# A mixer kernel in one launch: weight pieces in two transfers, a small score chunk on 128 queries, and a new order

## Chip, cores and metric

The kernel runs on one core of one Trainium2 chip. The metric is the device time of one execution in microseconds (us). One core has five engines that run beside each other, each in the order of its own instructions: TensorE (PE, matmuls; its weight loads are listed as PEld), VectorE (DVE), ScalarE (ACT), GpSimd (POOL) and SyncE (SP, which here only issues transfers, "DMAs"). They wait for each other by semaphores. PSUM is the memory that PE writes to; it has 8 banks.

## What is computed

Four batches of 448 tokens of width 768 go through causal attention with 12 heads of 64, then a token and channel mixer, then a gated unit:

```python
scores = where(causal, (q @ k.T) / 8, -1e9)            # 4 x 12 heads, 448 x 448
x = softmax(scores) @ v                                # to (4, 448, 768)
u = x + (relu(x.T @ w_tok1) @ w_tok2).T                # 448 -> 256 -> 448, over tokens
x = u + relu(u @ w_ch1) @ w_ch2                        # 768 -> 1536 -> 768
h = relu(x @ w_in); a, v = halves(h)                   # 768 -> 1024
v = (v - mean(v)) / sqrt(var(v) + 1e-6)
out = (a * (w_spatial @ v + b_spatial)) @ w_out        # 512 -> 768
```

All of the mixer's weights arrive as 64-bit floats and are narrowed to 32 bits on the chip.

## The kernel before

Two heads make a pair; there are 24 pairs, six to a batch. `scores(n)` multiplies the queries and keys of pair n in four chunks of queries, 0 to 64, 64 to 192, 192 to 320 and 320 to 448, each against the keys up to its end; the two heads lie on the two halves of the 128 rows of PE and run side by side. Pairs 0 to 5 (`whole`) multiply in float32 straight from the loaded `stage`; the others split queries and keys into a high and a low part (`qh`, `ql`) and take three products. DVE subtracts the row's maximum and masks, ACT takes the exponential and its sum, DVE the reciprocal, POOL scales; PE transposes the result (`transposed`), ACT or DVE copies it out of PSUM (`PT`), and `weighted(n)` multiplies by the values into `pso`, which ACT or DVE copies into U. After every third pair `token_mix` transposes half of a batch's U (`psm<-ident,U`, steps x0 to x3), splits it (`xs`) and runs the two token products.

The channel weights are 24 pieces of 128 x 768 numbers (`wch`, units of `UNITS`). `convert` loads a piece from DRAM as 64-bit words into one of three buffers (`way`); `narrow` turns it into float32 in three DVE steps for each half of 384 columns, through a PSUM bank; the result goes back to DRAM (`plain`), and `load_unit` fetches it again, when its use comes near, into one of four buffers (`whl`), where ACT and POOL split it into a high and a low part. The first three pieces are split straight from `way`. Batches 0 and 1 use these units one by one (`ch1`, `ch2`); batches 2 and 3 go together, by seven products in place of eight (`channel_pair`, `seven`). The gated unit's last step, `project`, also uses `seven`: for each block of outputs, products o = 0 to 6 that accumulate in three PSUM banks; what stands in a bank after each is copied or added into the `gate` buffers (`gather`), and finished blocks are stored (`out_t<-gate`, L1397).

Nothing of this runs in the order of the source. Each step is a `job` with its engine, a planned duration, what it reads and writes, a priority, and for PE an extra (`lead`); a search, which is not in the file, has used these numbers to order the jobs, and the file holds only its result: `ORDER` has a place for each job, with one bit that moves it to its other engine (ACT or DVE), and `BANKS` the PSUM bank of each product. `Plan.order` replays that table. The planned durations themselves are read by nothing at run time. So an edit of a duration shows only through the table.

The last product of all is cut in two:

```python
if tail and o == 6 and z == len(us) - 1:
    for half, c in enumerate(HALVES):
        job("PE", 0.66, partial(mms, c=c), ...)
        done(z, o, ps, half)
```

and at the start two filler matmuls on the mask (L1427) keep PE at work while the first softmax is under way.

Of the kernel before, what the change touches and what calls it, by code (L numbers as in the profile page):

```python
# [35 lines left out]
for q in range(4):  # L36
# [44 lines left out]
    "UISkPZv(soz5~AlU;||Xf&+sCVFO|VWCMf)$OFp*%maY~ivx@UmjjpsnFE>wn*-tl`2+d`h6A?)xC6NZodcc&p99SU<^%l${sWu?)C1K6)&s!<!UN6&*8>3r1q22J#RJ&`+5_7I+ymVM=>zHm4FoU*"
    "F$CBHJ_J7mKm_mu^#k?;K?FhsUIbqR3IGfM4FD4W6aWwa5daqe82}sr9sm{q7yuFg6#yCl9RMHzBLE)&CjcS<DgY$_CIB@6L;yDcKL8E@o&aM2WB^3~Mu0#7L4ZO4Ljausp@16zApj%*DF844I{+>K"
    "EC4tFG5{z5F#t9IJOD2MEdV(HGXO^bN&ra!OaM&)P5?*%SO7}^D*)91v;eh$ZUAq9f&ha6gaCzr#sJ3v1^`b0SpZT1Rsd80Pyk#2U;tkLS^!f3R{&K2Q2<^5VE|$PTL5qXaR7DzcK~t#bpUe!cmQ+&"
    "T>$$4u>iAxp8%kMuK=)sq5z`+`2hL=0RaL50|74qFaa?E{s8{~00A5U9RW)LL;+3#Q2}ZJG675hO#xy7i~)@SlmV3im;spq2moaOc>rnvXaHsaYyf=#dH{O>e*kL$X#i&cZ2*A)d;o?3fB=;MnE;yr"
    "oB)^rmjIRkngGxMegGB$(*V=}$N<Rz(E!o_$^gp%6af_hhXAAihyaWLi2#lOrvRn^ssN<`iU5rOivW)RtpKb5s{p6~)&SQ4+W^@B-T>SH-2mDE*Z`>jb^!zd1p)j3{QxZiE&)#gPyuuSbpf^jya2iY"
    "!vMJew*bNby#T-fzW}=c%m6b1xBxT(#Q?+r!2mS@IsrHVHvv2WHUT{WIRQHXz5uTQcL8|;cmbRNodKQ!t^u=wv;nmN-2t`%w*k!oxB<BV&;iZ?&jH^7-T~kN^8xe$^#S$)_W}3;5CRbb2?7cN6ap0j"
    "t^mydvH%MK&j1er4FL=R4gvT87Xb+Y9sxxG69GX1Mgc+r7y$|a9|3Cta{+7tash7vaRF`tZ2@or&H&i~qXDG>q=B#jvH`IH*a7kZ1_1{F-vBBBAOS}KD*;IXECC|{UI9`8ApuAMLjg(wQ~_WCUjb7A"
    "A_2Vt!~w$r!U4Yl!2!hqz5&1i2mu@d`2qR?`vLp`{sH{~8Uh;v5CIVZV*!N$XaQ#dW&vaYrUAwQh5?8H+5yr5X#r&crvb?UhXK(6=>h5i>jCcp>;dfo@B!`t@c|M6R{|sgCITe_O9D&+Py$f`RRV+p"
    "g#v~GfdYa8g92{?Z~}1xegc02fC9q;!~(?v$pXIuzyiSn!UD?z=>p6G`U1)V^#VQtKLMWs#{mukp#h))CjvbJ9Re!?DFP1yq5-@CC;~nL9s(=^Dgr+OMFK+tLIOboMgm6yL;^qpKmo@BYyxe9ZUUnM"
    "r2?b^#sbI!i2;fMVFFD8W&&gaX98jZhXPXqP6AH?XaZ#d-vVO-hyqpuR02{0-~!_U<pSga<^tgY=K|;g;sT2S90T_P_yYL?5d#tf69XCp8w1Dz$^oVVuL7z9tpcb5rvkGAvI4gPumY?Ct^%n7s{*zH"  # L90
    "wF1!sv;yt|@d85w^a33N@&fPz^8)Vz4FWv`9s?kQ9|J@KM*~I!N&`#-O#@B?PXkZ`Q3F&1QUg;1RRdN7R|8lBYXfWpZ3Auta077zbpv(-dIP5ecmt9HcLR9?ngW{w6ax_i7y~2&76TOn7X%sv6a*6l"
    "83QE)7Xy|9A_N-*6$BOpBLpV|Bm^l0B?K!3CIl)3C<L4We*{+qS%g>wWdvu0XoP+QfP}FExB^83G6YKlNCQa&lLI&eHUu*SIRqR8zynAGlmj~iHv~KcIs{1sPXtQ@O$1B?N(4~^P6SW{xdN{Qmjsvu"
    "ngoFaf&_zvtpu)w5(F3oW(02pZ3JrscLZq!cm#0-as+b(ZUk%ujRa~0c?5O@djxa@js%tjl?0Fkk_40lkpzzflLQ$A^#sBM!vw?x%LL2>&V=0r<pkyg=LF~k=>+No>jVx34+Rhf5d{(j69qK|HU&2Y"
    "I0aM%RRvZBR|Sd%iv{)t_XW@e(FHUFH3XRip#+`;pah!)oCK%@rv#$}r39Y@tOU6Podl``sRX11rUbeKzXZDkzy!Pm!36dMy#&4ldITT^2n7rU3x)Rt`2_d`9t9r-a0GP()&$K2*97bY*aX@H)CAK6"
    "(FD%~+yw0e*#z4J)dc$l(ge^1`~?0400jgE0tEpD0|oyC{RD{w#|0t<BLyS{SOr-HS_N+fbA_S=s{{!J76lvyJOwNT3I!Pj7X>B-8U-B%Jq0ZVE(IY47zHN<8wEZELIp+zL<K(uLj^?zKm|bs`UK<!"
    "a0PM&bp>|?fCY91bOm??aRq?|f(3*Hg9W7p;{^Z)G6qZrO$G%91_lQP0R{pF0|o>J2nHqwP6kf~VFqFbPzHtuhX#lSG6ypUzXret)&|!GIR!ceTLobST?J|dUIknQZ3ScnWd&jdU<GRhYz1EhZUtur"
    "W(8vfrUkJDs0FJ9uLY+Cv<0dKtOYv-I0mx?sRgnHum!gTwgt5Xtp%<HxCP|}=LO~k=mj(eQHC!CFa?qYn+1~vmj##wl?9yzp9P!+paql#ngy8!mIa;#qXnS_qy^~(?*;P(@dfw=>jmls76$GGF$J3j"
    "@CEe+^ac3^@&)V#?FASH7X}*!HU>8aH3m`!mIj;#Xa#8n(goTD)dklD(*@K8+XdeR;04_U)&<xFIR^g)+y&wV;RW6WItDxjKL$MpLIyhqMg~3xL<YtM(gs5YK?XnuU<OGBNCrm+Y6e9HYX+AFnFg2!"
    "ng-7X(1rsC1P28N-3HzU-v-(S+XmbQ4+jtj5eGO2IR`oiI|nugHwQciJqJz)PX|>8RtH1}MF*k<2?h`b3kDMgS_TmY6$T6j4h9+q83q&vTLuyabOsFu4+b*^Wd?Nyeg=64cLsq5cm{d~d<J#~3I+=Y"
    "od$gde+GgEfCh~Qdj^9Btp=_J)CSWA)dtZ91_um>Fa|LO#s*3T$Og;?$_B><Xa-{jYzA!x$p*~^&IZc{X$E8l<OXgA<p$~o@CNP%><04&=LYBo<_7Bq@&@q+?*{b-^acS3=?3iv0tW~O2L}oV2?s|9"  # L100
    "RELBHg$AAmrv{(~p$4A@q6Vl2s|K$Iu?D6FqXwl0qz0)5tOl?K6bBUt7zZ8)B?lJ=76%#!AO|7`83!K+AqOT090wZ*9S0)^BnKx4Ne4;?O$SH^X$NWtaR+q=b_Z++Z3k`#cL#U}c?W9;ZwGJ(iwBGc"
    "jR%eghX;rUi3f@Ypa-D`m<O2$)d$)KjscGWmI0Rm+X37G5&{zf3jz!R76LK?HUc*SNCHU$N&<2Ma{_b%bpmz*d;)y}i~@}U%>pd~E&?+GGy*jOodTW$p8}u)p#tgx>jLZo?E(Y?CIcq}F9R?G&I0xV"
    "1p@~IEdwqCJOe!gJ_A1kX9H*hX#<S|jsuSakpry*p#!1=qXVP^rUSAAvjcPkl>@p1-UGV>y#vMr#{<Iy!~@9#$^+j6-~-_U;{)Ua<pbvf=mYTs@&o?^00aUA_XGF?3<M4Y4+IbdECekCLj*(wE(9+G"
    "U<6?VMg&I$V+3RbiUf=V#{|d(w*<HZ$^?7_eFXah`~&j?^aBF~1O!|JT?ASLTLeV}umrIL;{@ac1qB8L2L)mT#RSF#^91w+G6gdQGzE(UM+Ha)j0KGajs=eekp;;F6a^IpP6bZ|Pz6#2Qw0qLdj)(2"
# [136 lines left out]
def mixer_kernel(ctx: ExitStack, tc: tile.TileContext, qkv, wtok, wch, wgv, wsp, bsp, out):  # L241
# [145 lines left out]
    def nominal(n):  # L387
        return 0.0 if n < EAGER else START + (n - EAGER) * STEP
# [1141 lines left out]
```

## Time and profile before

| what | us |
|---|---|
| median of 3 runs (lowest, highest) | 756.04 (755.39, 758.48) |
| the profiled execution | 756.18 |
| its span, first to last instruction | 754.4 |
| PE busy | 741.0 (98%) |
| DVE busy | 635.8 (84%) |
| ACT busy | 419.4 (56%) |
| POOL busy | 293.0 (39%) |
| transfers: 122.06 MB, mean 162 GB/s | |

Busy time is the time in which at least one instruction of an engine runs. Matmuls overlap, so what one costs on PE is the distance from its start to the next one's start, not its duration. Idle time is listed beside the instruction that ended it, with what it had waited for ("<-").

### The profile page before, as it was taken

Reading aid. Unit: us, or ns where it says so; the run is one execution under the profiler, and the core shown is the slowest. Engines: PE = TensorE matmul, PEld = TensorE weight load, DVE = VectorE, ACT = ScalarE, POOL = GpSimd, SP = SyncE. Lnnn points to the kernel's source line nnn. Section 1 sums busy time; section 2 is a strip of 40 time slices with the busy share of each in tenths; the row PEclk is TensorE's granted clock in tenths of the full one; section 3 lists DMA queues with packets and bytes.
Section 4 is the critical chain, followed back from the end, with each engine's and each line's share of the span. In section 5 each row is a group of like instructions: output and inputs, shape, how many; then the busy total and the mean of one; then the engine's idle time right before and its main releaser. Section 6 shows DMA issues by size and latency. Waiting matters only on the chain. (4 is left out here: it accounts for less than half of the span.)

```text
span 754.4 us, 12904 instructions
## 1 busy us (share of the span) xinstructions
PE 741.0 (98%) x4450; PEld 635.6 (84%) x4450; DVE 635.8 (84%) x1529; ACT 419.4 (56%) x1025; POOL 293.0 (39%) x361
## 2 busy tenths in 40 slices
PE   9999999999899999999999999999999999999998
PEld 4667888789778888888799999999888988889997
DVE  6999999988797787776599889999999998789773
ACT  6998665243577865553246567545465655554441
POOL 5789647234695767736120000000430112542600
PEclk9999999999999999999999999999999999999999
DMA  6458879879677879797624402223201011200123
GB/s 246 144 197 283 264 250 325 294 249 330 230 248 242 258 257 341 216 274 221 208 91 141 144 2 84 84 103 129 76 23 43 0 43 50 85 0 13 49 98 135
DMA packets 48754, 122.06 MB, mean 162 GB/s; under 512 B 4912, under 2 KB 20400, under 8 KB 48176
## 3 DMA queue, kind: packets, MB, share of 16 engines
q1 hardware_dynamic: 48688, 121.23, 48.7%
q8 instruction: 35, 0.57, 0.3%
q14 instruction: 31, 0.25, 0.1%
HBM read 91.46 MB, written 29.75 MB: 161 GB/s over the span
## 5 line engine op out<-in xcount | busy, mean ns | idle before, releaser
L298 PE MATMUL psf<-fb,fa 128*128 128x448 f32 (+1 forms) x422 | 154.6, 366 | 1.1 <-DVE U L1091 0.6
L300 PE MATMUL psf<-fb,fa 128*128 128x448 f32 (+1 forms) x422 | 154.4, 366 | 0.1
L299 PE MATMUL psf<-fb,fa 128*128 128x448 f32 (+1 forms) x422 | 154.4, 366 | 0.0
L289 POOL TENSOR_TENSOR whl<-whl 128x768 fp32r<-128x768 f32 x45 | 82.9, 1852 | 102.3 <-ACT whl L818 82.0
L488 ACT ACTIVATE P<-P,stats 128x320 f32<-128x320 f32 (+3 forms) x192 | 96.0, 503 | 31.4 <-DVE stats L471 30.5
L509 POOL TENSOR_SCALAR P<-P,stats 128x320 f32<-128x320 f32 (+3 forms) x192 | 87.4, 473 | 29.9 <-DVE stats L500 26.2
L298 PEld LDWEIGHTS psf<-fb,fa 128*128 128x128 f32 x422 | 79.2, 188 | 9.2 <-issue 1.0
L937 ACT CAST fa<-raw 128x384 fp32r<-128x384 f32 (+1 forms) x112 | 55.9, 531 | 54.0 <-DVE raw L951 23.6
L300 PEld LDWEIGHTS psf<-fb,fa 128*128 128x128 f32 x422 | 79.3, 188 | 7.4 <-DVE fa L289 0.4
L299 PEld LDWEIGHTS psf<-fb,fa 128*128 128x128 f32 x422 | 79.3, 188 | 7.3
L471 DVE CUSTOM_DVE_ANT_0 P<-pss,mask 64x64 f32<-64x64 f32 (+3 forms) x192 | 70.2, 413 | 9.6 <-PE pss L462 8.8
L289 POOL TENSOR_TENSOR wv<-wf,wv 128x512 fp32r<-128x512 f32 x6 | 8.5, 1425 | 154.0 <-ACT wv L1167 154.0
L289 DVE TENSOR_TENSOR fa<-raw,fa 128x384 fp32r<-128x384 f32 (+1 forms) x109 | 59.7, 572 | 5.2 <-ACT fa L937 4.6
L298 PE MATMUL ps<-hid,whl 128*128 128x448 f32 x144 | 54.2, 376 | 0.0
L818 ACT CAST whl<-whl 128x768 fp32r<-128x768 f32 x45 | 37.0, 832 | 30.4 <-DMA whl<-plain 28.8
L300 PE MATMUL ps<-hid,whl 128*128 128x448 f32 x144 | 52.8, 367 | 1.0 <-POOL whl L289 1.0
L298 PE MATMUL ps<-uhl,whl 128*128 128x448 f32 x144 | 53.6, 372 | 0.0
L300 PE MATMUL ps<-uhl,whl 128*128 128x448 f32 x144 | 52.7, 366 | 0.0
L299 PE MATMUL ps<-uhl,whl 128*128 128x448 f32 x144 | 52.7, 366 | 0.0
L299 PE MATMUL ps<-hid,whl 128*128 128x448 f32 x144 | 52.7, 366 | 0.0
L901 ACT CAST fb<-U 128x448 fp32r<-128x448 f32 x57 | 31.5, 565 | 27.6 <-DVE U L906 16.6
L289 POOL TENSOR_TENSOR ql<-stage,qh 128x896 fp32r<-128x896 f32 x18 | 38.1, 2120 | 7.6 <-ACT qh L396 7.2
(182 smaller groups left out, 1786.7 us busy)
## 6 DMA issues: line engine op xcount, KB each, us to landing
way<-in_wch SPq DMA_DIRECT2D x24, 768.0 KB, 6.3
whl<-plain SPq DMA_DIRECT2D x45, 384.0 KB, 5.2
stage<-in_qkv SPq DMA_DIRECT2D x23, 448.0 KB, 4.2
plain<-way SPq DMA_DIRECT2D x24, 384.0 KB, 5.0
raw<-plain SPq DMA_DIRECT2D x24, 384.0 KB, 3.6
round<-PB SPq DMA_DIRECT2D x7, 1024.0 KB, 6.1
PT<-round SPq DMA_DIRECT2D x28, 256.0 KB, 5.2
v<-in_qkv SPq DMA_DIRECT2D x24, 256.0 KB, 4.6
```

Of the source, the lines that this page charges most:

```text
L289: e.tensor_tensor(lo, x, hi.bitcast(F32), op=ALU.subtract)
L298: nc.tensor.matmul(ps, ah, bh, start=(first and i == 0), stop=False, **kw)
L299: nc.tensor.matmul(ps, ah, bl, start=False, stop=False, **kw)
L300: nc.tensor.matmul(ps, al, bh, start=False, stop=(last and i == n - 1), **kw)
L471: nc.vector.tensor_tensor_reduce(out=P(i)[:M, j, :], in0=ps(i, j), in1=mask[:M, S - 128 : S - 128 + W] if j == 0 and n < BLOCKS or M == 64 ...
L488: nc.scalar.activation(P(i)[:M, j, :], P(i)[:M, j, :], AF.Exp, bias=s.t[:M, 0, c : c + 1], scale=-1.0, accum_out=sums(s)[:M, c, 0:1])
L509: nc.gpsimd.tensor_scalar(P(i)[:M, j, :], P(i)[:M, j, :], s.t[:M, 1, c : c + 1], 1.0, op0=ALU.mult, op1=ALU.mult)
L818: job("ACT", act(DM, False), lambda: nc.scalar.copy(w.t[:, 0, :], w.t[:, 1, :].bitcast(F32)), r=ks, w=ks, prio=p)
L901: job("ACT", act(S, False), lambda: nc.scalar.copy(f(0), x_()), r=wk, w=[(h, k, 0)], prio=p)
L937: job("ACT", act(n, False), lambda: nc.scalar.copy(part(o, 0), at(d)), r=[key(d)], w=[wk], prio=p + 0.1 * o)
```

## The change

1. `wch` is laid out as two contiguous halves of 384 columns per piece, and `convert` loads a piece of channel weights in two transfers, one for each half (768 KB becomes 2 x 384 KB). The narrowing of a half now depends on its own transfer alone. Both transfers wait until both halves of the buffer's last contents have been narrowed (`ends`). The token weights' pieces stay whole.
2. In the pairs with float32 scores the chunk of 64 queries is multiplied with 128 queries (`wide`): 64 rows of the result are not read by anything.
3. The last product is whole again, and only ACT's copy of it and its store are cut in halves.
4. Planned durations and leads of the score jobs and of some transposes are lowered, and the search was run again: `ORDER` and `BANKS` are new throughout. 32 jobs take their other engine in place of 38; six copies go from DVE to ACT. The transfers rise from 307 to 331.

```diff
 ORDER = (
-    "4*&oF0RRF31ONj71po&C@Br}u^Z*(G8v*M8>;UZm?f~xq2>>(zIslLWkpPqc;sE0S<pAaY83B?2lK|iV;Q-_S3jpT;=m6;e>HzWp^#Jw&BmpJ?Cjs{WC;=$}RRMzmgaK9oR{>Z7Spi)ETmka{TLEDK"
+    "4*&oF0RRF31ONj71po&C?f~xq^Z*wD83E}4>HzBi>;UZm2>>(zegLTessOD3-~izO;{fCUG6AaqtN`8s-vHtO3jpN+<^bma=m78l^#Jw&9|0l(BLVjS4FMzpB>`3eR{>Z7SpixBTLD}FVF6$P@c<41"
...
 BANKS = (
-    "777777777777777777777773333333333333333333333333333333345021354654021354655021346654544546564021364566021366655021364566645464654021354545021375645021"
+    "777777777777777777777773333333333333333333333333333333345021356555021366455021346454464556645021354646021356454021365466654464546021354545021364574021"
...
-    def narrow(d, dk, w, wk, n, prio, banks=(3,)):
+    def narrow(d, dk, w, wk, n, prio, banks=(3,), ends=()):
...
-            job("DVE", (n * 1.04 + 70) / 1e3, lambda k=k: step(k), r=[dk, (ps, 0)] if k else [dk], w=[wk] if k == 2 else [(ps, 0)], touch=[wk[0]], prio=prio)
+            job("DVE", (n * 1.04 + 70) / 1e3, lambda k=k: step(k), r=[dk, (ps, 0)] if k else [dk], w=[wk, *ends] if k == 2 else [(ps, 0)], touch=[wk[0]], prio=prio)
...
-        n = src.shape[-1]
-        dk = (b, "d")
-        job("SP", 0.385, lambda: nc.sync.dma_start(b.t[:, : 2 * n], src.bitcast(U32)), w=[dk], prio=prio, size=n * 1024, lead=0.29 if n == DM else 0.415)
+        if isinstance(src, tuple):
+            for k, x in enumerate(src):
+                job("SP", 0.385, lambda k=k, x=x: nc.sync.dma_start(b.t[:, 2 * HALF * k : 2 * HALF * k + 2 * HALF], x.bitcast(U32)), r=[(b, "ends", x) for x in (False, True)], w=[(b, "d", k)], prio=prio + 0.1 * k, size=HALF * 1024, lead=0.34)
+        else:
+            n = src.shape[-1]
+            job("SP", 0.385, lambda: nc.sync.dma_start(b.t[:, : 2 * n], src.bitcast(U32)), w=[(b, "d", 0), (b, "d", 1)], prio=prio, size=n * 1024, lead=0.29 if n == DM else 0.415)
...
-        def ps(i, j):
+        def ps(i, j, wide=False):
             k, o_ = PLACE[i]
-            M, W = CHUNKS[i][1] - CHUNKS[i][0], CHUNKS[i][1]
+            M, W = 128 if wide else CHUNKS[i][1] - CHUNKS[i][0], CHUNKS[i][1]
...
+                wide = whole and i == 0
+                if wide:
+                    q1 = 128
...
-        for some, us in (((3, 0), 1.214 if whole else 0.86), ((2, 1), 1.065 if whole else 0.86)) if n else (((0, 1), 1.1), ((3,), 0.85), ((2,), 0.85)):
+        for some, us, lead in (((3, 0), 1.075 if whole else 0.776, 0.0 if whole else 0.08), ((2, 1), 0.97 if whole else 0.838, 0.0 if whole else 0.02)) if n else (((0, 1), 1.0, 0.0), ((3,), 0.85, 0.0), ((2,), 0.85, 0.0)):
...
-        convert(i % 3 if i < 6 else 1 + i % 2, wch[i], parts, LOW + i, (7,) if i < 8 else (3,), keep=i)
+        convert(i % 3 if i < 6 else 1 + i % 2, (wch[i, 0], wch[i, 1]), parts, LOW + i, (7,) if i < 8 else (3,), keep=i)
...
                 if tail and o == 6 and z == len(us) - 1:
-                    for half, c in enumerate(HALVES):
-                        job("PE", 0.66, partial(mms, c=c), r=[us[z][1](o), *((*place[o][i][:2], x) for i in range(n) for x in range(2)), *([("tail", 0)] if half else ())], w=[(ps, half), ("tail", half)], prio=base + 0.01 * o)
+                    for half in range(2):
                         done(z, o, ps, half)
...
+    wch = wch.reshape(24, 128, 2, HALF).transpose(0, 2, 1, 3)
```

How the table moves PE's instructions is shown at three places (a row is a line, an operation, output<-inputs by their names, and the output's size; x2 is two alike in a row). First PE at the scores of pairs 2 and 3 (`stage_145` and `stage_149` are their operands, `pst` a bank of transposes). Before:

```order
L462 MATMUL pss<-stage_145 128x448 x2
L462 MATMUL pss<-stage_145 64x64 x2
L462 MATMUL pss<-stage_145 128x320 x2
L462 MATMUL pss<-stage_145 128x192 x2
L547 MATMUL pst<-ident,P_69 128x128 x2
L547 MATMUL pst<-ident,P_187 128x128 x2
L462 MATMUL pss<-stage_149 128x448 x2
L462 MATMUL pss<-stage_149 64x64 x2
L547 MATMUL pst<-ident,P_70 128x128
L547 MATMUL pst<-ident,P_212 128x128 x3
```

The same place on PE now:

```order
L468 MATMUL pss<-stage_145 128x448 x2
L468 MATMUL pss<-stage_145 128x64 x2
L468 MATMUL pss<-stage_145 128x320 x2
L468 MATMUL pss<-stage_145 128x192 x2
L468 MATMUL pss<-stage_149 128x448 x2
L468 MATMUL pss<-stage_149 128x64 x2
L553 MATMUL pst<-ident,P_187 128x128 x4
L468 MATMUL pss<-stage_149 128x320 x2
L468 MATMUL pss<-stage_149 128x192 x2
```

The small chunk's output grew from 64 x 64 to 128 x 64, and pair 3's first scores now follow pair 2's without transposes between them.

Second, PE at the last token mix of the second batch (`pso` is the weighted product of the batch's last pair, `U_1178` and `U_1184` the batch's U, `ps_2056`, `ps_2108` and `ps_2152` banks of channel products). Before:

```order
L679 MATMUL pso<-PT,v 64x384 x2
L679 MATMUL pso<-PT,v 64x64 x2
L684 MATMUL pso<-PT,v 64x384 x2
L684 MATMUL pso<-PT,v 64x256 x2
L684 MATMUL pso<-PT,v 64x128 x2
L740 MATMUL psm<-ident,U_1178 64x128 x3
L740 MATMUL psm<-ident,U_1178 128x128 x9
L298 MATMUL ps_2056<-uhl,whl 128x448
```

The same place on PE now:

```order
L690 MATMUL pso<-PT,v 64x384 x2
L690 MATMUL pso<-PT,v 64x256 x2
L690 MATMUL pso<-PT,v 64x128 x2
L298 MATMUL ps_2108<-hid,whl 128x448
L299 MATMUL ps_2108<-hid,whl 128x448
L300 MATMUL ps_2108<-hid,whl 128x448
...
L746 MATMUL psm<-ident,U_1184 128x128 x9
L746 MATMUL psm<-ident,U_1184 64x128 x3
L298 MATMUL ps_2152<-uhl,whl 128x448
```

A channel product of nine matmuls now stands between the weighted product and the transposes of what it makes.

Third, the end of PE's order, with buffer numbers (`psf_7971` is, before and after, the bank whose product o = 6 is the one with two copies). Before:

```order
L300 MATMUL psf_8082<-fb_7799,fa_7459 128x448
L298 MATMUL psf_7971<-fb_7980,fa_7449 128x224
L299 MATMUL psf_7971<-fb_7980,fa_7449 128x224
L300 MATMUL psf_7971<-fb_7980,fa_7449 128x224
L298 MATMUL psf_7971<-fb_7999,fa_7449 128x224
L299 MATMUL psf_7971<-fb_7999,fa_7449 128x224
L300 MATMUL psf_7971<-fb_7999,fa_7449 128x224
...
L1526 UNCONDITIONAL_BRANCH
```

The end of PE's order now:

```order
L300 MATMUL psf_7971<-fb_8018,fa_7469 128x448
L298 MATMUL psf_8074<-fb_7843,fa_7479 128x448
...
L300 MATMUL psf_8074<-fb_7830,fa_7479 128x448
L298 MATMUL psf_8021<-fb_7843,fa_7479 128x448
...
L300 MATMUL psf_8021<-fb_7830,fa_7479 128x448
L298 MATMUL psf_8134<-fb_7750,fa_7349 128x448
...
L300 MATMUL psf_8134<-fb_7855,fa_7349 128x448
L1532 UNCONDITIONAL_BRANCH
```

The product with the two copies is now the fourth from the end; the last is one that DVE adds to `gate` as a whole.

## Rows read from the trace of the kernel before

**Rows 1.** The page, part 1: busy us (share of the span) and instructions of each engine.
```profile
PE 741.0 (98%) x4450; PEld 635.6 (84%) x4450; DVE 635.8 (84%) x1529; ACT 419.4 (56%) x1025; POOL 293.0 (39%) x361
```

**Rows 2.** Waits of PE: who waited for whom, us in total, times, longest.
```profile
PE psm L740 <- ACT U L688: 1.3, 2, 0.6
PE ps L300 <- POOL whl L289: 1.0, 1, 1.0
PE pso L679 <- ACT PT L579: 0.9, 3, 0.3
PE pss L462 <- DVE gw L317: 0.9, 1, 0.9
PE psm L766 <- ACT PT L551: 0.7, 1, 0.7
PE psf L298 <- DVE U L1091: 0.6, 1, 0.6
...
PE psm L740 <- DVE hid L292: 0.2, 1, 0.2
```

**Rows 3.** Stretches: us; busy us (instructions) by engine; clock, DMA share, GB/s.
```profile
40.00:60.00 20.00, 18.17 (x154) 13.91 (x153) 18.17 (x66) 18.94 (x60) 16.52 (x23) 1.00 0.64 206
...
180.00:200.00 20.00, 19.00 (x99) 16.71 (x97) 16.48 (x31) 8.49 (x14) 12.45 (x9) 1.00 0.82 295
```

**Rows 4.** Order of time, PE and PEld, pair 2's scores: start, us, instruction.
```profile
14.12 0.65 PE L462 MATMUL pss<-stage 64*128 64x448 f32 x2
...
15.07 0.14 PEld L462 LDWEIGHTS pss<-stage 64*64 64x64 f32 x2 [0.65 <-issue]
...
15.33 0.30 PEld L462 LDWEIGHTS pss<-stage 64*128 64x128 f32 x4
15.33 0.19 PEld L462 LDWEIGHTS pss<-stage 64*128 64x128 f32 x2
...
16.39 0.14 PEld L547 LDWEIGHTS pst<-ident,P 128*128 128x128 f32 x1 [0.23 <-ACT P L488]
```

**Rows 5.** Order of time, PE, from plain matmuls to transposes.
```profile
146.60 0.37 PE L299 MATMUL ps<-uhl,whl 128*128 128x448 f32 x1
146.80 0.37 PE L300 MATMUL ps<-uhl,whl 128*128 128x448 f32 x1
147.10 0.65 PE L565 MATMUL pst<-ident,P 64*128 64x64 f32 x14
```

**Rows 6.** Order of time, the second batch's last token mix.
```profile
151.78 1.17 PE L740 MATMUL psm<-ident,U 128*64 128x128 f32 x9 [0.63 <-ACT U L688]
...
153.44 0.55 PE L740 MATMUL psm<-ident,U 128*128 128x128 f32 x3 [0.49 <-DVE xs L289]
```

**Rows 7.** Order of time, the end.
```profile
749.03 0.27 PE L298 MATMUL psf<-fb,fa 128*128 128x224 f32 x1
...
749.23 0.62 DVE L1006 TENSOR_TENSOR gate<-psf,gate 128x448 f32<-128x448 f32 x1 [0.59 <-PE psf L300]
...
750.33 0.37 PE L298 MATMUL psf<-fb,fa 128*128 128x224 f32 x1 [0.48 <-ACT gate L998]
...
750.99 0.27 PE L300 MATMUL psf<-fb,fa 128*128 128x224 f32 x1
751.29 0.34 ACT L998 COPY gate<-psf 128x224 f32<-128x224 f32 x1 [1.02 <-PE psf L300]
```

**Rows 8.** Transfers: issues by line, KB each, median us to landing.
```profile
way<-in_wch SPq DMA_DIRECT2D x24, 768.0 KB, 6.3
...
raw<-plain SPq DMA_DIRECT2D x24, 384.0 KB, 3.6
...
out_t<-gate SPq DMA_DIRECT2D x23, 224.0 KB, 1.9
...
out_t<-gate SPq DMA_DIRECT2D x2, 112.0 KB, 1.7
```

**Rows 9.** Instructions on way: ns min/median/max, first and last start us.
```profile
L346 SPq DMA_DIRECT2D way<-in_wch x24: 327/402/1462, 34.9 to 186.2; - x24
```

More of the change, by code (lines that the diff above doesn't have):

```diff
@@ L81 @@
[L81 to L92, printed above, removed]
@@ L132 @@
+    "M+`^|UJPIiVGLpnV+@fDQ4CWIUkri_nhbmleGGmKJPbVyRt#?pXAFZ3gbalYhYX4gOAJg5k_?j!nGA*un+%)`O$<&9a13z_atw|Pj|`U#m<*o`pbVi5qYR`Br3|PHsSK(NQVfs`hzyAguMDsZu?)ow"
+    "#tg>{oeZ9gt_-(~rVOVHq71SO!VJR<#0<X-zzo3*s|>6RtqijaxD31uv<$TjwhXxpy$rq#x(vGvIsiKW"
 )
 BANKS = (
[L134 to L135 removed]
@@ L138 @@
+    "135021356475646656764456757764467565745675566576565577546456575467747446744754455464674473333333333333333333333607124375260154637201463752014375260073"
+    "1436210567201657435176717226517257460712435646177201546376"
 )
@@ L352, in w @@
                 return b.t[:, o : o + m].bitcast(F32)
-            narrow(lambda c0=c0, c1=c1: b.t[:, 2 * c0 : 2 * c1], dk, w, wk, c1 - c0, prio, banks)
+            narrow(lambda c0=c0, c1=c1: b.t[:, 2 * c0 : 2 * c1], (b, "d", int(c0 >= HALF)), w, wk, c1 - c0, prio, banks, [(b, "ends", c0 >= HALF)])
             if hi is None:
@@ L567, in transposed @@
                 keys = [k for ks, _ in some for k in (ks if isinstance(ks[0], tuple) else (ks,))]
-                job("PE", 0.52 - 0.03 * g, mms, r=keys, w=[(ps, 0) for ps in halves], touch=[t], prio=n, mode=1)
+                job("PE", 0.52 - 0.03 * g, mms, r=keys, w=[(ps, 0) for ps in halves], touch=[t], prio=n, mode=1, lead=0.0)
                 for r, ps in enumerate(halves):
@@ L997, in gather @@
             other = "DVE", dve(S // 2), lambda: nc.vector.tensor_copy(h()[:, c], ps.t[:, c])
-            job("ACT", act(S // 2), lambda: nc.scalar.copy(h()[:, c], ps.t[:, c]), r=[(ps, half)], w=[(*hk[0], half)] if half else hk, prio=prio, other=other)
+            job("ACT", act(S // 2), lambda: nc.scalar.copy(h()[:, c], ps.t[:, c]), r=[(ps, 0)], w=[(*hk[0], half)] if half else hk, prio=prio, other=other)
             return
@@ L1029, in seven, with mms @@
                 ps = banks[z][k]
-                def mms(o=o, z=z, ps=ps, first=first, c=slice(0, S)):
+                def mms(o=o, z=z, ps=ps, first=first):
                     w = us[z][0]
-                    mm3(ps.t[:, c], [(w(o, 0, i), w(o, 1, i), place[o][i][2](0)[:, c], place[o][i][2](1)[:, c]) for i in range(n)], first=first, skip_group_check=True)
+                    mm3(ps.t[:, :S], [(w(o, 0, i), w(o, 1, i), place[o][i][2](0), place[o][i][2](1)) for i in range(n)], first=first, skip_group_check=True)
                 after = []
@@ L1042, in seven @@
                     after += start
+                job("PE", (0.0, 0.0, 1.216, 1.842)[n], mms, r=[*after, us[z][1](o), *((*place[o][i][:2], x) for i in range(n) for x in range(2))], w=[(ps, 0)], prio=base + 0.01 * o)
                 if tail and o == 6 and z == len(us) - 1:
-                    for half, c in enumerate(HALVES):
-                        job("PE", 0.66, partial(mms, c=c), r=[us[z][1](o), *((*place[o][i][:2], x) for i in range(n) for x in range(2)), *([("tail", 0)] if half else ())], w=[(ps, half), ("tail", half)], prio=base + 0.01 * o)
+                    for half in range(2):
                         done(z, o, ps, half)
-                    continue
-                job("PE", (0.0, 0.0, 1.216, 1.842)[n], mms, r=[*after, us[z][1](o), *((*place[o][i][:2], x) for i in range(n) for x in range(2))], w=[(ps, 0)], prio=base + 0.01 * o)
-                done(z, o, ps)
+                else:
+                    done(z, o, ps)
     def channel_pair(b0, b1):
```

102 lines of the change are left out of this document (55 added, 47 removed).

## The prediction

> **What bounds the kernel now.** I read the page first: the span and the engines' busy time. TensorE (PE) is busy 741.0 us of 754.4, the next engine, DVE, 635.8 [rows 1]. So a change can only help by making TensorE's stream shorter, by removing its idle time, or by shortening what stands ahead of its first and behind its last instruction. The granted clock is 1.00 in the stretches read below [rows 3], so I expect nothing from the clock. Second view: who made PE wait. Behind the wait ahead of its first instruction, that view has 14 rows, from 1.3 down to 0.2, which add up to 8.1 us [rows 2]. That is all that a better order can win inside the program, about 1.1%. Third, the stretches: in 40 to 60 us PE is busy 18.17 of 20, and DVE (18.17) and ACT (18.94) are just as full; in 180 to 200 PE has 19.00, with DMA at 0.82 [rows 3]. So the waits lie where attention, token mixing and the weights' conversion share the engines. Fourth, I read two stretches in order of time for what a form of matmul costs, and the end [rows 4 to 7].
>
> Times are made against the profiled execution: 756.18, which is its span of 754.40 and 1.78 around it. It lies 0.14 above the median of the three runs, 756.04, so 0.14 is taken off at the end.
>
> **Scores on 128 queries.** Before, the small chunk's matmuls use a 64 by 64 corner of the array between two 64 by 128 neighbours. In the pair shown, the 448-column matmuls start at 14.12, the small ones at 15.07, the next 320-column ones at 15.33, and the job after at 16.39 [rows 4]. The small ones wait until the array is empty: their weight load stood idle 0.65 on "issue". The (3, 0) job thus takes 15.33 - 14.12 = 1.21 and the (2, 1) job 1.06. With one form throughout, a load can run beside the matmul ahead of it: four 64 by 128 loads of 0.19 are done in 0.30, so a pass follows the pass ahead by (0.30 - 0.19) = 0.11. Two passes on two heads side by side then cost 0.22, and the next job starts at about 15.18 in place of 15.33: 0.14 saved. The 320-column passes behind also start without the change of form; I give that half as much, 0.07. So 0.21 for each pair. Six pairs have float32 scores; the first two lie ahead of the first transposes, where PE has filler matmuls anyway, and I count nothing for them. Four pairs: 4 x 0.21 = 0.84, taken as 0.9 with a bit for the first start. Bounds: nothing (0.0), if the loads of 128 columns stay in sight, and 6 x 0.26 = 1.6, if the whole stretch of 0.26 from 15.07 to 15.33 vanishes.
>
> Against this speaks a rule of the Trainium skill, in "TensorE: Matmul & The Clock Gate", section on LDWEIGHTS: a load takes time by its columns, about columns / 1.2 ns, whatever the rows. By it a load grows by some 53 ns (an estimate from that page), and 4 pairs x 4 loads x 0.053 would eat 0.85 of the gain, so the total would come out near 753.4. The trace agrees that the wide load is longer (0.19 against 0.14), but shows the loads of two heads side by side, so I leave the sum as it is.
>
> **Fewer changes of form.** Where PE goes from plain matmuls to transposes, the next start comes 0.30 after the last (146.80 to 147.10), against about 0.20 within plain matmuls [rows 5, 7]. Runs of one kind on PE number 145 in the order before and 136 in the new one. 9 x 0.10 = 0.9; some changes cost less, so 0.7, between 0.0 and 0.9.
>
> **The end.** Before, the last product is cut in halves of columns. The first half starts at 749.03; the second waits 0.48 for ACT's copy of the first and starts at 750.33; its last matmul starts at 750.99, ACT copies from 751.29 for 0.34, and a 112 KB store follows [rows 7]. In the new order the last product is whole, and another one: it feeds a DVE addition and a store of 224 KB. Six matmuls 0.20 apart starting at 749.03 begin the last at 750.04, in place of 750.99: -0.95. Six matmuls of 448 columns end 0.10 later past their start than those of 224 (0.37 against 0.27): +0.10. DVE's 0.62 stands in place of ACT's 0.34: +0.28; the store takes 1.9 in place of 1.7 [rows 8]: +0.2. Sum -0.37; I take -0.3, between -0.9 (if the 0.28 and 0.2 overlap) and +0.5 (if the final chain cannot start on time). The copies in halves that remain have three products behind them, 3.6 us of cover.
>
> **Waits that the new order takes up.** PE's wait of 0.63 at 151.78 is for ACT's copy of U, since the transposes stand right behind the product that it copies; the 0.49 at 153.44 is for DVE's xs three transposes later [rows 6]. In the new order nine matmuls, 9 x 0.20 = 1.8, stand between the product and the transposes: both waits go, -1.1. For the first token mix (the 0.7 on PT before L766 [rows 2]), the order around it moved too; I count half of it and of what follows, -0.5. The other of the two waits for U (1.3 in all [rows 2]) lies behind the fourth batch's last product and stays at 0.67: there the same rows stand before and after. Sum -1.6. The other waits (8.1 less 0.48 at the end, 1.6, and 0.67, so 5.4) are queues that meet by chance: the POOL split of a weight block 1.0, the narrowing of gw on a score's bank 0.9, U's additions 0.6, PT copies 0.9 [rows 2]. Each hangs on an order that was redone everywhere; I take them as neither better nor worse: 0, between -5.4 and +4 (half as many again as there are now).
>
> **The split transfers.** 24 issues become 48, all on SP: 24 x 0.40 = 9.6 us of SP's time in the 151 us between 34.9 and 186.2 [rows 9]. Bytes are equal. DVE can narrow a half when it lands, some 3 us sooner; it is the load's own wait on DVE that this would take away, and PE shows no wait on it [rows 2]. Cover: the pieces stand in line ahead of PE's use. Cost 0; if that cover is gone see the slower rival. Six copies go from DVE to ACT; neither bounds by itself: 0.
>
> **Sum.** -0.9 - 0.7 - 0.3 - 1.6 = -3.5; 756.18 - 3.5 = 752.7, less 0.14: 752.5.
>
> **Rivals.** *The queues' waits go as well.* DVE loses six copies and can start on a half that has landed, so that what queues behind it is freed sooner; of the 5.4 us of chance waits half go, -2.7: 749.8. For it: they are the only large sum left. Against it: PE, DVE and ACT are all near full in 40 to 60, and POOL has 16.52 of 20 [rows 3].
>
> *The waits form again elsewhere.* PE's stream gets shorter by 1.9, but DVE and ACT are as full as PE in 40 to 60 [rows 3], and what PE saves there it waits for: the 1.6 returns, 754.1; if the scores' 0.9 returns too, 755.0.
>
> *Slower: the second halves come late.* Place: SP's queue and the DMA rings, 35 to 190 us, DMA share 0.64 to 0.82 [rows 3]. A 768 KB piece lands in 6.3; a 384 KB one from DRAM in 3.6, so two one after the other take 7.2, 0.9 more [rows 8]; and each second issue costs 0.40, with the loads of stage, v and whl queued behind it on SP. If each piece slips by that 0.40, the last is 24 x 0.40 = 9.6 later and the channel matmuls wait for weights as at the 1.0 for whl, time and again: 762.1. It decides from a slip of 0.30 per piece, where 7.2 has eaten the gain and 0.5% more. Against it: PE waited on whl once, for 1.0, in the whole program [rows 2]. A rule speaks for it, in "DMA: Bandwidth & Descriptors", section "Anatomy of one DMA": about 2.0 us of each transfer are fixed. No row here shows it as queue time.
>
> *No effect at all*: the new order does what it did, and only the form and the end change: 756.04 - 1.2 = 754.8; it lies in the second rival's case.
>
> **How the numbers follow.** What a measurement of this kernel can tell is about 0.5%, 3.78 us: faster is below 752.26, slower above 759.82. Forecast (0.55): 752.5, own range 750.8 to 754.5; the bound cuts it, 0.23 below and 0.32 above. Queues' waits go (0.20): 749.8, faster. Waits form again (0.16): 754.1 to 755.0, same. Late halves (0.09): 762, slower. So faster 0.43, same 0.48, slower 0.09. The range goes from 749.0 (a bit under the first rival) to 756.8 (over the second); left out are the late halves and the ends of the two rivals.
>
> **What would show it.** Scores: no 0.65 on "issue" ahead of the small chunk's loads, and about 1.07 from one 448-column start to the 320-column one. The end: no wait of L998 on PE, a DVE addition and a 224 KB store last. Waits: no PE wait for U near 143 to 152 us, the one of 0.6 behind the last product of the fourth batch still there; the sum of PE's waits 5 to 6.5 in place of 8.1. Transfers: pairs of 384 KB within 6 to 7 us, PE waits on whl not above 1. The forecast is wrong if PE's waits add up to over 8, or if its busy time is not 1 to 2 us less.

## The result, and the profile after

749.84 us is the median of 5 executions (748.59 to 749.99); the kernel before took 757.36 beside them (755.39 to 758.48, 5 executions). The ratio is 0.9899, 95% interval 0.9878 to 0.9921. Measured twice more beside other executions of before, the ratio was 0.9931 (0.9907 to 0.9955) and 0.9940 (0.9916 to 0.9963), with medians of 749.72 and 749.85. So the changed kernel stays at 749.8, and what moves is the kernel before, whose single executions lie between 752.4 and 759.1. The gain is 4.6 to 7.5 us. Forecast were 752.5 and a range of 749.0 to 756.8: the time is inside the range, on the value of the first rival (749.8) and not on that of the forecast.

Part 1 of the page after, the span and each engine's busy time, against [rows 1]:

```profile
span 748.2 us, 12957 instructions
PE 735.2 (98%) x4444; PEld 636.4 (85%) x4444; DVE 630.4 (84%) x1523; ACT 419.7 (56%) x1031; POOL 292.0 (39%) x361
```

PE's busy time fell by 5.8 and its idle time hardly (754.4 - 741.0 = 13.4 before, 748.2 - 735.2 = 13.0 now). A second trace of before has 738.4 busy, two more of the changed kernel 735.0 and 736.6, so by the means the fall is 4.1. Either contradicts the forecast's own test, 1 to 2 us less busy. The waits of PE after (who waited for whom, total us, times, longest), against [rows 2]:

```profile
PE zeros L1439 <- DVE P L1435: 1.4, 1, 1.4
PE pso L669 <- DMA PT<-round: 1.4, 1, 1.4
PE psm L772 <- DVE xs L289: 1.2, 1, 1.2
PE ps L298 <- DVE U L864: 0.8, 1, 0.8
PE pss L468 <- DVE stats L477: 0.7, 1, 0.7
PE psm L746 <- ACT U L694: 0.6, 1, 0.6
...
PE pss L468 <- DMA stage<-in_qkv: 0.4, 1, 0.4
```

Without the start they add up to 7.3, where 5 to 6.5 had been forecast. The waits for whl (1.0), gw (0.9) and the tail's gate copy (0.5) are gone, one of the two for U also; new are, above all, those for PT<-round, for xs in the first token mix, and for stage.

The four places of which the prediction spoke, each in order of time (start, us, instruction). The scores of pair 2, PE and its weight loads, against [rows 4]:

```profile
14.32 2.11 PE L468 MATMUL pss<-stage 64*128 64x448 f32 x16 [0.39 <-DMA stage<-in_qkv]
14.78 0.22 PEld L468 LDWEIGHTS pss<-stage 64*128 64x128 f32 x2 [0.15 <-issue]
15.15 0.98 PEld L468 LDWEIGHTS pss<-stage 64*128 64x128 f32 x10 [0.15 <-issue]
...
16.68 0.61 PE L468 MATMUL pss<-stage 64*128 64x448 f32 x1 [0.25 <-PE pss L468]
```

Before, the same 16 matmuls, from the first start to the last end:

```profile
14.12 2.35 PE L462 MATMUL pss<-stage 64*128 64x448 f32 x16
```

The loads stand idle 0.15 ahead of the small chunk in place of 0.65, and the pair's 16 matmuls are over in 2.11 in place of 2.35. But two new waits, 0.39 and 0.25, stand around them.

The second batch's last token mix, against [rows 6], and the fourth batch's:

```profile
147.33 0.36 PE L300 MATMUL ps<-hid,whl 128*128 128x448 f32 x1
147.53 1.60 PE L746 MATMUL psm<-ident,U 128*128 128x128 f32 x12
...
369.50 0.77 PE L746 MATMUL psm<-ident,U 128*128 128x128 f32 x5 [0.63 <-ACT U L694]
```

The twelve transposes run without a wait, where 0.63 and 0.49 had been; the wait behind the fourth batch's last product stayed at 0.63. The end, against [rows 7]:

```profile
743.16 0.36 PE L298 MATMUL psf<-fb,fa 128*128 128x448 f32 x1
...
744.17 0.36 PE L300 MATMUL psf<-fb,fa 128*128 128x448 f32 x1
744.57 0.62 DVE L1012 TENSOR_TENSOR gate<-psf,gate 128x448 f32<-128x448 f32 x1 [0.59 <-PE psf L300]
```

From the last product's first matmul to the end of the span it was 754.40 - 749.03 = 5.37 and is 748.21 - 743.16 = 5.05. The transfers, against [rows 8]:

```profile
way<-in_wch SPq DMA_DIRECT2D x48, 384.0 KB, 5.2
...
raw<-plain SPq DMA_DIRECT2D x24, 384.0 KB, 3.7
...
out_t<-gate SPq DMA_DIRECT2D x23, 224.0 KB, 1.9
```

A pair of halves takes 6.6 (median of 24) from the first issue to the second landing, where the whole piece took 6.3. PE never waits for `whl`.

**An account of PE's steps.** Because the listed waits do not explain the gain, I took, from the trace, the step from each PE instruction to the next start, less the wait listed there, less what such an instruction takes in the middle of a run of its own kind (the mean of the shorter four fifths of such steps; 0.2027 for a 448-column matmul). Before has two traces (spans 754.4 and 753.7), the changed kernel three (748.2, 747.5, 749.3); the columns are means in us. Single rows hang on what is taken for the middle of a run: with one common mean for all five traces they move by up to 0.6, and the steps between kinds fall by 2.2.

| where on PE | before | after | difference | forecast |
|---|---|---|---|---|
| listed waits | 9.2 | 7.1 | -2.1 | -2.1 (1.6 and the tail's 0.5) |
| the rest of the step at a wait | 4.6 | 3.8 | -0.8 | none |
| steps from one kind of work to another (144, now 135) | 14.8 | 12.5 | -2.35 | -0.7 |
| inside float32 scores | 4.6 | 4.0 | -0.6 | -0.9 |
| inside the later pairs' scores | 7.0 | 6.0 | -0.9 | none |
| short waits inside plain matmuls, 0.07 to 0.26 each, not listed | 1.8 | 0.7 | -1.1 | none |
| behind PE's last matmul | 3.4 | 4.0 | +0.6 | +0.2 (the end's -0.3 without its wait of 0.5) |
| spacing of plain matmuls, 206.7 against 202.7 ns | 2.4 | 3.5 | +1.2 | none |
| inside transposes and all else | | | +0.4 | none |
| span | 754.1 | 748.4 | -5.7 | -3.5 |

### The profile page after: what moved, and what is told of

The parts are those of the page before. It is cut to its first block, busy times and chain, and to the rows that moved or that the text cites. A ratio compares the mean times of both kernels' runs of the same rounds, so it can differ in the third digit from the quotient of the medians.

```text
span 748.2 us, 12957 instructions
## 1 busy us (share of the span) xinstructions
PE 735.2 (98%) x4444; PEld 636.4 (85%) x4444; DVE 630.4 (84%) x1523; ACT 419.7 (56%) x1031; POOL 292.0 (39%) x361
## 4 chain that ended last, share of the span: by engine, by line
PE 79%; DVE 6%; DMA 3%; issue 1%; ACT 0%; SPq 0%; DVEq 0%; ACTq 0%
PE psf L300 11%; PE psf L299 11%; PE psf L298 11%; PE ps L298 6%; PE ps L299 6%; PE ps L300 6%; PE psv L298 3%; PE psv L299 3%; PE psv L300 3%; PE pss L468 2%; PE psm L298 2%; PE psm L299 2%; PE psm L300 2%; PE pso L669 2%; DMA gw<-in_wgv 2%; PE psp L300 1%
## 5 line engine op out<-in xcount | busy, mean ns | idle before, releaser
L298 PE MATMUL psf<-fb,fa 128*128 128x448 f32 x420 | 153.7, 366 | 0.0
L299 PE MATMUL psf<-fb,fa 128*128 128x448 f32 x420 | 153.7, 366 | 0.0
L300 PE MATMUL psf<-fb,fa 128*128 128x448 f32 x420 | 153.6, 366 | 0.0
L494 ACT ACTIVATE P<-P,stats 128x192 f32<-128x192 f32 (+3 forms) x192 | 96.1, 502 | 30.5 <-DVE stats L477 29.7
L515 POOL TENSOR_SCALAR P<-P,stats 128x448 f32<-128x448 f32 (+3 forms) x192 | 87.4, 474 | 41.4 <-DVE stats L506 35.7
L477 DVE CUSTOM_DVE_ANT_0 P<-pss,mask 128x192 f32<-128x192 f32 (+3 forms) x192 | 70.3, 414 | 11.3 <-PE pss L468 10.8
```

The source lines that it names most:

```text
L298: nc.tensor.matmul(ps, ah, bh, start=(first and i == 0), stop=False, **kw)
L299: nc.tensor.matmul(ps, ah, bl, start=False, stop=False, **kw)
L300: nc.tensor.matmul(ps, al, bh, start=False, stop=(last and i == n - 1), **kw)
L477: nc.vector.tensor_tensor_reduce(out=P(i)[:M, j, :], in0=ps(i, j), in1=mask[:M, S - 128 : S - 128 + W] if j == 0 and n < BLOCKS or M == 64 ...
L494: nc.scalar.activation(P(i)[:M, j, :], P(i)[:M, j, :], AF.Exp, bias=s.t[:M, 0, c : c + 1], scale=-1.0, accum_out=sums(s)[:M, c, 0:1])
L515: nc.gpsimd.tensor_scalar(P(i)[:M, j, :], P(i)[:M, j, :], s.t[:M, 1, c : c + 1], 1.0, op0=ALU.mult, op1=ALU.mult)
```

## Experiments

**Order and edits apart.** Two kernels, each traced and timed twice. One replays the old table with all three edits (the second transfer of a piece right behind the first, the whole last product in the place of its first half). The other replays the new table without the edits.

```diff
+            if j.behind is not None:
+                j.start = j.behind.start + 1
+                continue
...
-            j.start = r & 32767
+            j.start = 4 * (r & 32767)
```

> The old order with all three edits: float32 scores' small chunk on 128 queries, pieces in two transfers (the second issued right behind the first), last product whole. Theory A (the gain is the new order): only the scores' 0.9 to 1.3 us and 0.3 at the end, so 1.2 to 1.6 us less than before, ratio about 0.998; PE's waits of 0.97 for whl near 197 us and 0.90 for gw near 205 us stay. Theory B (halves that land early free the queues): those two waits go as well, 3.2 us or more less, ratio 0.996 or below. Theory C (second halves late, the slower rival): ratio above 1.005, with waits for whl.

> The old order with the three edits, again: its first trace gained 2.7 us over the kernel before, of which 2.8 was spacing (130 slow matmuls in place of 825) and the rest scores against new waits. If the edits alone are worth 1.2 to 1.6 (theory A), a second trace with another count gives a span of 751.2 plus 4 ns for each slow matmul, within 1.0.

> The new order without the three edits (64 queries, pieces in one transfer at the place of whichever half stood first, last product in halves). Theory A: most of the gain stays, 5.5 to 6.5 us less than before, ratio 0.9915 to 0.993. Theory B: the order needs the early halves, PE waits for weights or for banks near 180 to 210 us, 3 us or less gained, ratio 0.996 or above.

> The new order without the edits, again. Theory A: 5 to 6 us below the kernel before in its span (753.7 to 754.4), and the two stretches of slow spacing as in the changed kernel. Theory F (edits and order gain only together): 3 us or less.

| | ratio to before (95%) | span | spacing's part | span without it |
|---|---|---|---|---|
| before | | 754.4, 753.7 | 3.4, 1.3 | 751.0, 752.4 |
| old order, edits | 0.9964 (0.9947 to 0.9981), 0.9978 (0.9960 to 0.9996) | 751.7, 752.9 | 0.5, 3.5 | 751.1, 749.4 |
| new order, no edits | 0.9959 (0.9941 to 0.9977), 0.9973 (0.9955 to 0.9992) | 748.6, 751.4 | 2.7, 2.7 | 745.9, 748.7 |
| changed kernel | 0.9899, 0.9931, 0.9940 | 748.2, 747.5, 749.3 | 3.0, 3.0, 4.6 | 745.2, 744.5, 744.8 |

Without the spacing the edits alone are worth 1.4, the order alone 4.4, both 6.9; two traces of one kernel differ there by up to 2.8. By the medians (752.84, 752.53; 752.19, 753.34; before 755.54, 754.43) it is 1.9 to 2.7 and 1.1 to 3.4. Both are gains by themselves, and the order is the larger one in the traces; by the times the two can't be told apart. Theory A's 1.2 to 1.6 for the edits holds in the mean of the spans; its ratio of 0.998 only in the second run, since the first trace had 130 matmuls at the wider spacing against 825 and so looked 2.8 better. The order's 5.5 was a little too much. Theory B falls in the main: in the old order the wait for `whl` stays at 0.7 and 0.6 although the halves land early. But the wait for gw near 205 us (0.9 and 1.0 in the two traces of before), which theory A wanted to stay, is gone in both, so there the edits did take up one wait. Which edit did it was not tried; the new order has no such wait with or without them. The slower rival falls too. The waits are not what the order alone settles either: 6.7 in one execution of it and 8.3 in the other, with a wait of 1.8 for PT<-round in the second.

**One transfer, and 64 queries, in the new order.** In the first the piece is loaded whole, where the first of its halves was; in the second `wide` is off.

```diff
-                wide = whole and i == 0
+                wide = False
```

> The changed kernel, only that a piece comes in one transfer, issued where the first of its two halves was issued, in the old layout. Theory A: no difference to the changed kernel that can be measured, 749.3 to 750.5 us (ratio to before 0.990). Theory B: 2 to 3 us slower than the changed kernel, ratio 0.993, with new PE waits behind narrowing between 40 and 210 us.

> The changed kernel, only that the small chunk of the float32 scores is multiplied with 64 queries again. If the prediction's term holds at its place and reaches the end: 0.9 to 1.3 us slower than the changed kernel, about 751 us. Rival: PE spends what it saves there on waiting for the loads and for the softmax of the first pairs (the changed kernel's waits of 0.39 for stage, 0.25 for pss and 0.35 for P before 17 us), then 0.3 us or less.

Medians 750.39 and 750.44, ratios 0.9938 (0.9913 to 0.9962) and 0.9935 (0.9912 to 0.9957). Neither differs by more than the intervals from the changed kernel's 0.9931 and 0.9940, so in the new order whether the halves land early is worth nothing that can be measured, and the scores' 0.6 to 0.9 is below what the times resolve here. The spans, 752.3 and 750.9, look worse, but 4.9 of the first is spacing, and each has other chance waits (1.6 for xs; 2.3 for U, which in the changed kernel's three traces is 0.8, 0.2 and 0.5). By their times these two runs are inconclusive. For the scores the place itself decides: with 64 queries the 16 matmuls of pair 2 take 2.35 again, and the jobs of pairs 2 to 5 take 0.6 more than in the changed kernel. Two places where wider passes follow the corner inside the pair give 0.19 and 0.22 of it, two where another kind of work follows 0.07 and 0.09. From the start of pair 2 to the end of pair 5 it is 15.63 in this run and in both traces of the new order without edits, and 15.27 in the changed kernel's three: of the 0.6, 0.36 is left, and waits take the rest.

**The price of a change of form.** 66 products of `seven` get a guest ahead of them that writes into the bank that the product then overwrites: once a matmul of 64 columns with the product's own operands, once a transposition of a 64 x 64 corner.

```diff
                     w = us[z][0]
+                    if first:
+                        nc.tensor.matmul(ps.t[:, :64], w(o, 0, 0), place[o][0][2](0)[:, :64], start=True, stop=True)
```

> The changed kernel with a guest of the same form as its neighbours (128 rows, 128 x 64 out) ahead of 66 products of seven; its result is overwritten by the product. It is the base for the next run: each guest adds one matmul's step, at most the 0.20 of a full one and at least the 0.19 of a weight load, 12 to 13.5 us in all on PE. Theory D: 206.7 and 202.7 both occur again, in other stretches.

> As guest_same, but the guest is a transposition with a 64 x 64 corner. The prediction's price (0.10 for each run of one kind): an excursion and back costs 0.2 beyond the guest's own 0.04, so 66 x 0.24 = 16 us more than the changed kernel. The account of the changed kernel's trace (0.09 on the way in, 0.13 on the way out, 0.10 at the first matmul behind): 66 x 0.36 = 24 us more than the changed kernel.

One execution each: 755.74 and 771.86 us, 6.0 and 22.1 above the changed kernel's 749.72 beside them. PE in order of time, with the guest of the same form:

```profile
448.63 0.37 PE L300 MATMUL psf<-fb,fa 128*128 128x448 f32 x1
448.84 0.19 PE L1040 MATMUL psf<-fb,fa 128*128 128x64 f32 x1
448.87 0.44 PE L298 MATMUL psf<-fb,fa 128*128 128x448 f32 x1
449.15 0.36 PE L299 MATMUL psf<-fb,fa 128*128 128x448 f32 x1
```

and with the transposition, PE, then its weight load:

```profile
451.00 0.37 PE L300 MATMUL psf<-fb,fa 128*128 128x448 f32 x1
451.30 0.24 PE L1040 MATMUL psf<-ident 64*64 64x64 f32 x1
451.47 0.47 PE L298 MATMUL psf<-fb,fa 128*128 128x448 f32 x1
451.77 0.36 PE L299 MATMUL psf<-fb,fa 128*128 128x448 f32 x1
```

```profile
451.29 0.10 PEld L1040 LDWEIGHTS psf<-ident 64*64 64x64 f32 x1 [0.31 <-issue]
```

Over all 66 the three steps around a transposed guest have medians of 0.298, 0.172 and 0.310, where two steps of 0.203 would stand: 0.374 more. Less the 0.03 that one such transposition takes inside a run (two start every 0.06), an excursion costs 0.34, 0.17 for each change. It is in three parts: 0.10 ahead of the guest, whose load stands idle 0.31 on "issue"; 0.14 behind it; and 0.10 at the next load. This is the price of leaving plain matmuls and coming back. The guest of the same form adds 0.11 (means 0.206, 0.030 and 0.284). The forecast's 0.10 saw only the first part. My account's 24 us against 16 is borne out: 66 x 0.374 = 24.7, of which 1.5 came back because fewer steps were at 206.7 ns (366 against 739); that is 1.1 more than the measured 22.1, and the listed waits of this one execution, 5.5, are 1.3 below the 6.8 of the changed kernel beside it. For the guest of the same form I had expected 12 to 13.5; it was 7.5 by its steps, since its load runs beside the matmul ahead of it.

**Is the spacing drawn anew?** The same two programs again, unedited.

> The kernel before once more, unedited. Theory D: a count other than 825 at 206.7 ns, the stretch from 403 to 532 us no longer slow or slow with other ends, and a span that moves by 4 ns for each. Theory E: the same stretches, 825 within 50. PE's listed waits at the same places in either case, 8.1 us within 0.5.

> The changed kernel once more, unedited. In the first trace of it 729 of some 2080 plain matmuls that stand in steady streams are 206.7 ns apart and the others 202.7 ns; in the kernel before, 825 of 2035. Theory D (spacing is drawn in each execution at a weight load that had to wait, and lasts until the next such load): another count here, anywhere from 100 to 1500, a span that differs from 748.2 by about 4 ns for each matmul more or less, and the slow stretch from 380 to 455 us is gone or has another end. Theory E (the spacing belongs to the program): the same stretches and 729 within 50. Time: 0.990 of the kernel before.

> The changed kernel a third time, as the corner of a two by two on one chip: order and edits. Ratio 0.990 to 0.993. If the slow spacing belongs to the program in this order (both traces of it so far have 120 matmuls at 206.7 ns from 157 us and 364 from 379 to 454 us), those two stretches are there again.

The stretch from 410 to 530 us (490 to 530 in the first trace of the changed kernel) holds nothing but 448-column matmuls. Their groups (line, form, count; busy us, mean ns), in the first trace of before, then in the second:

```profile
L298 PE MATMUL psf<-fb,fa 128*128 128x448 f32 x194 | 71.4, 368 | 0.0
```

```profile
L298 PE MATMUL psf<-fb,fa 128*128 128x448 f32 x198 | 72.3, 365 | 0.0
```

and in the changed kernel from 410 to 450, and from 490 to 530 (us; busy us and instructions of PE, PEld, DVE, ACT, POOL; granted clock, DMA share, GB/s):

```profile
410.00:450.00 40.00, 40.00 (x196) 36.32 (x195) 33.88 (x67) 24.54 (x53) 0.00 (x0) 1.00 0.19 65
490.00:530.00 40.00, 40.00 (x199) 37.07 (x198) 39.49 (x77) 20.13 (x43) 2.55 (x2) 1.00 0.27 94
```

The same instructions, at the same granted clock of 1.00, follow each other either 206.7 or 202.7 ns apart. In before the wide spacing covered 825 steps in the first trace and 283 in the second; the stretch from 403 to 532 was gone. In the changed kernel it covered 729, 739 and 1124: the stretches from 157 and from 379 us are there in all three, and in the third a further one, from 455 to 549. So neither theory holds alone: some stretches come with the order, others with the execution. Where the spacing changed for long within a run of plain matmuls, in all fourteen traces here, a weight load had stood idle just there for 38 ns or more, where loads in the stream stand idle 9 to 20. The end of before's second trace is not better by the 2.2 us that 542 steps are worth, since its listed waits were 2.1 longer (10.2; I had expected 8.1 within 0.5).

**A version that beats both.** In the run with 66 guests of the same form the spacing was 202.7 ns behind every guest in the channel products. So three of them, ahead of the products where the wide spacing held on for long:

```diff
+                if next(at_ch2) == 6:
+                    guest(ps, w.t[:, 0, cs[0]], hs[0].t[:, 0, :])
...
+                    if start and o == z == 0:
+                        guest(ps, w(o, 0, 0), place[o][0][2](0))
```

(and one more of the first kind in `ch1`.)

> The changed kernel with three guests of 64 columns in the form of their neighbours, ahead of the products at 157, 184 and some 395 us, each overwritten by its product. In the run with 66 of them every guest left the spacing at 202.7 ns behind it. If that is so here: about 470 matmuls go from 206.7 to 202.7 ns, 1.9 us, less 3 x 0.11 for the guests: the span is 1.6 us below the changed kernel's 747.5 to 748.2. If the spacing falls back by itself or is decided by the order: 0.3 us slower.

747.36 us median (746.87 to 749.29, 6 executions), ratio to before 0.9909 (0.9885 to 0.9933), beside 749.85 of the changed kernel: 2.5 less. Its span is 745.5, and 189 steps are at the wide spacing. The change is seen at the third guest:

```profile
392.87 0.37 PE L303 MATMUL psf<-fb,fa 128*128 128x448 f32 x1
393.08 0.37 PE L304 MATMUL psf<-fb,fa 128*128 128x448 f32 x1
393.29 0.37 PE L305 MATMUL psf<-fb,fa 128*128 128x448 f32 x1
393.49 0.19 PE L295 MATMUL psf<-fb,fa 128*128 128x64 f32 x1
393.52 0.44 PE L303 MATMUL psf<-fb,fa 128*128 128x448 f32 x1
393.81 0.36 PE L304 MATMUL psf<-fb,fa 128*128 128x448 f32 x1
394.00 0.36 PE L305 MATMUL psf<-fb,fa 128*128 128x448 f32 x1
```

Steps of 0.21 ahead of it, 0.20 behind it. Forecast were 1.6 less; the spacing's part in the span fell from 3.0 to 4.6 in the three traces of the changed kernel to 0.8. Not all of the gain is spacing: the listed waits, 6.4, are 0.4 to 0.9 lower than in those three.

## Why the prediction was right in its range and wrong in its size

**The bound** was right: PE is busy 98% after as before, and every term of the gain is on PE.

**Scores on 128 queries** (-0.9): right in mechanism, the stall on "issue" fell from 0.65 to 0.15. At pair 2 the size was right too: 0.24 for its 16 matmuls against a forecast of 0.21, and 0.99 from the first 448-column start to the 320-column one (14.32 to 15.31), where 1.07 was forecast and 1.21 stood before. But not every pair has it whole: the four pairs give 0.6, since the corner costs less where another kind of work follows it, and 0.36 of that is left behind pair 5. The rest goes into waits, as the second rival had it for all of it. The wider loads of 128 columns do not show: by the rule of the Trainium skill that was weighed there ("TensorE: Matmul & The Clock Gate", LDWEIGHTS) four pairs would have lost 0.85; the trace does not agree, the whole pair got shorter.

**Fewer changes of form** (-0.7, at most -0.9) is the step that failed. The number, 9, was right as a number of kinds of work (144 steps from one kind to another, now 135). But the price goes with the form, the two numbers joined by * in a row, which say what part of the array an instruction uses, and not with the kind. In each of the five traces of the account a step between kinds that changes the form costs 0.13 (0.129 to 0.133) beyond such a step inside a run, and one that keeps it costs nothing (-0.01 to -0.02). The rows show both: from plain matmuls to 64*128 transposes 0.30 (146.80 to 147.10 [rows 5]), from plain matmuls to 128*128 transposes 0.20 (147.33 to 147.53 above). In PE's order the steps between kinds that change the form fell from 115 to 103; those without a listed wait fell from 108 and 107 to 93, and 14.5 x 0.13 = 1.9 of the account's 2.35. The rest, 0.4, I have not taken apart. So 9 was too few, and the price of 0.10 too low: it was read where plain matmuls are left, which costs 0.09 on average, and leaving a narrower form costs 0.12 to 0.18. The guests' 0.17 is not the price to put here: it holds the 0.10 at the next load inside the plain matmuls, and the new order leaves plain matmuls no less often (35 runs of them, now 36). The Trainium skill says in "TensorEngine Tiling (Array Packing)", Key Properties, that a change of tiling mode drains the engine; the traces agree in that a step costs extra only where the form changes, and the price of it here is the measured 0.13.

**Left out altogether**: the later pairs' scores, -0.9. Eight pairs now multiply chunks 2 and 1 first and go straight on to 3 and 0; before it was three. The small chunk's 64-row corner then stands at the end of the pair, where PE changes its form anyway (13 pairs in place of 11), and 23 separate groups of such scores are left of 26. That this makes the whole row is not shown: inside the pairs PE goes from the corner back to a wider pass 5 times in place of 7, and the row is -0.65 with the common mean. The lowered planned durations of these jobs were in the diff; they show only through the table, and I did not follow what the table made of these jobs.

**The end** (-0.3): right, 5.05 against 5.37.

**Short waits**, also left out: before has them at 666 to 670 us (four of 0.1 to 0.2) and at 700 (0.34), at operands that come a moment late, too short to be listed; after has none over 0.11. That is 1.1, and was there to be read in the steps of the trace of before. Which part of the new order took them away was not tried.

**Waits** (-1.6, and 0.5 at the end): the two of the second batch's last mix went, the fourth batch's stayed at 0.63, both as forecast. Of the first token mix half was to go; in place of 0.7 and 0.4 there stands 1.2. The chance waits were not neutral one by one: `whl` and gw left, PT<-round (1.4, 0.7 and 1.6 in the three traces) came; the second trace of before has 0.5 of it. The sum is right by the means, 2.1 with the tail's, and beyond the forecast a wait costs more than is listed: the rest of the step at each of them gave 0.8 more.

**The split transfers** (0) cost nothing that can be measured, and in the new order gain nothing: 6.6 for a pair against 6.3, no listed wait for `whl`, and the one-transfer run at 750.39. In the old order the wait for gw left with the edits. SP's queue and the fixed cost of a transfer, on which the slower rival rested, had no say; the section of the Trainium skill that it named gives the 2.0 us for transfers that GpSimd issues, while SP issues these, and the 112 KB stores land in 1.7 [rows 8].

**The first rival** gave the right time for another reason: of the chance waits some left and others came, and what the account has beyond the forecast (5.7 against 3.5) came out of PE's busy time: 1.65 more for the changes of form, 0.9 for the later scores, 1.1 for short waits and 0.8 next to listed ones, against 1.2 that the spacing took and 1.1 in small terms. This sum goes by the account; no run takes the terms of the new order one by one. By the sign that the prediction itself set, busy time 1 to 2 us less, the mechanism was too small.

## What to carry to other kernels

When an engine is busy 98%, look for the gain in the steps between its instructions and not in the listed waits: count the changes of the array's form and not of the kind of work (0.13 each here, nothing where the form stays), and price a new excursion from plain matmuls whole, in, out and the next load (0.34 here), before a new order is judged. A small matmul of another form costs least where another kind of work follows (0.07 to 0.09 in the float32 scores, against 0.19 to 0.22 between wider passes). Where two executions of one program differ by as much as the change is worth, take several traces and subtract what differs between executions before terms are compared.

## What was not expected of the hardware

A stream of identical fp32 matmuls of 448 columns with their loads has two spacings, 206.7 and 202.7 ns, at the same granted clock of 1.00, and keeps the one it has for hundreds of instructions, until a weight load is late or, as at the third guest, a shorter matmul stands in the stream. In this kernel that is 0.5 to 4.9 us of the span, which is as much as the edits, and it accounts for part of the scatter of one and the same program. A guest of 64 columns in the same form, at 0.11 us, always left the narrower one behind it in the stretches looked at, but only at one place, near 393 us, did the wide one stand right ahead of it, in both runs with such guests. Why there are two, and what chooses one when a run of plain matmuls begins, stays open: no run here tells it.
